# A mixture-of-experts kernel beside a spectral filter: the data's low part last in each product, and three low parts a unit formed by VectorE instead of GpSimd

## The chip, the cores and the metric

The kernel runs on one core of a Trainium2 chip. The metric is the time on the device in microseconds (us), the median of several runs. Five engines have queues of their own and run side by side: TensorE (PE; its weight loads are listed as PEld), VectorE (DVE), ScalarE (ACT), GpSimd (POOL) and SyncE (SP, which here issues transfers). An engine works through its queue in order.

## The reference

The input x has 2048 tokens of 512 numbers. The result is x + A(layernorm(x)) + B(layernorm(x)). A is a filter in the frequency domain, B a mixture of 8 experts in which each token uses all 8 (K = 8), weighted by its gates:

```python
def A(x, w_r, w_i):
    X = fft.rfft2(x) * (w_r + 1j * w_i)
    return fft.irfft2(X, s=(S, D))

def B(xt, wg, w1, w2):               # xt (2048, 512), w1 (8, 512, 1792), w2 (8, 1792, 512)
    gates = softmax(xt @ wg)         # top 8 of 8, normalised again
    h = gelu(einsum("nd,edf->nef", xt, w1))
    y = einsum("nef,efd->ned", h, w2)
    return einsum("ne,ned->nd", gates, y)
```

All arrays are fp32.

## The kernel before

**Exactness.** TensorE multiplies fp32r numbers, which carry fewer bits than fp32. Each operand is therefore split into a high part, rounded to fp32r, and a low part, the rest: ScalarE casts the high part, then VectorE or GpSimd subtracts it from the source (`high` and `low`, L983 and L988, for data; `split`, L682, for weights). A product of two operands takes three passes: low weights by high data, high by low, high by high. The tuple `PASSES` (L44) holds the order (1, 0), (0, 1), (0, 0), where 1 is the low part, the weights' index comes first and the data's second. `PASSES1` (L45) is (0, 0), (1, 0), (0, 1).

**Prologue.** The hidden dimension of each expert is cut into 7 chunks of 256, 56 chunks in all. The first two go through a plain scheme in the first 120 us (`mm1`, L708, with `PASSES1`, and `mm2`, L729, with `PASSES`), while the layer norm, the gates and the operands of the rest are prepared.

**Units.** The other 54 chunks are taken two at a time (27 pairs, index c), and the tokens in two halves (index i): 54 units, numbered u, in a loop (L1302). "Even" and "odd" units are those with i = 0 and i = 1. Each unit does both layers for its pair by Strassen's scheme in Winograd's form: 7 block products a layer instead of 8, with sums of blocks as operands. A block product (`product`, L946) is 256 x 256 weights by 256 x 512 data: for each of two column halves m, three passes by two k, so 12 matmuls of 512 columns. Each column half has a PSUM bank of its own. Three pairs of banks, A, B and C, take the results. Some products start afresh, others add to what is in the bank, and must wait until the result before has been read.

`layer1` (L992) is a generator for the first layer of a unit. It also finishes the unit before: it forms the weighted hidden blocks and their sums, and their high and low parts (tile hs, four buffers), that the second layer of that unit needs. `layer2` (L1134) does the seven products of the second layer, of the unit before, in the order b22, T3, b11, b21, T1, T4, T2, each followed by an addition of the result into acc on VectorE (`into`). T3 adds to b22's bank pair C, b21 to b11's bank pair B, and T4 to T1's bank pair C, each behind that addition. Hidden blocks and their sums lie in five buffers of the tile c (`tmp`, L975): o11, o21, o22 and o12 are those of the unit before, h11, s, h22 and h12 those of this one.

**Order.** A unit is seven steps n, each with one product of layer 1 (first `next(one)`), one of layer 2 (`next(second)`), and the small work between. Every instruction on TensorE, VectorE, ScalarE and GpSimd is pinned to the order in which it is written (`pin`). `weights(n)` puts the preparation of the next weights there: ScalarE casts them (tiles ua, us of layer 1, va, vs of layer 2), GpSimd forms their low parts and the sums of blocks (tiles s and raw), each a two-input instruction of 512 columns. The filter A is cut into small chunks that are put in between by `slot_pe` and `slot_dve`: matmuls into psf and VectorE work on the tiles Y, A, B, C, D of line 438 (names that PSUM's banks share by chance).

The data of layer 1 come from device memory (`xin`, tile xr), high and low parts together.

Before the change, in a unit: VectorE forms the low parts of T3 (step 0), T4 and T2 (step 2) and of b22 (step 6). GpSimd forms those of T1 (step 0), b21 (step 1) and b11 (step 3), by `low(..., True)`.

Of the kernel before, what the change touches and what calls it, by code (L numbers as in the profile page):

```python
# [19 lines left out]
P = 128  # L20
# [99 lines left out]
def body(ctx: ExitStack, tc: tile.TileContext, io):  # L120
    plain_order, strict, pinned = False, False, {}

    def pin(ins):
        if strict:
            engine = ins.ins.engine
            last = pinned.get(engine)
            if last is ins.ins:
                return ins
            if last is not None:
                tc.add_manual_dep(  # L130
                    ins.ins, last.name,
                    mybir.DependencyInfo(mybir.DependencyClass.NoSync, mybir.DependencyReason.DATA), reason="layout",
                )
            pinned[engine] = ins.ins
        return ins
# [593 lines left out]
    def mm2(q, t, w2, h):  # L729

        e = ORDER[2 * q] // NC
        for j in range(TB // P):
            js = slice(j * P, (j + 1) * P)
            p2 = ps2.tile([P, D], F32, name="p2")
            n = 0
            for f in range(2 * NFT):
                for hw, hh in PASSES:
                    nc.tensor.matmul(p2, h[f][:, hh, js], w2[f][:, hw], start=(n == 0), stop=(n == 6 * NFT - 1))
                    n += 1
            b = t * 4 + j  # L740
            early()
            nc.vector.scalar_tensor_tensor(
                acc[:, b, :], p2, cw[:, b, e : e + 1], acc[:, b, :], op0=ALU.mult, op1=ALU.add
            )
            tick()
# [199 lines left out]

    def product(pt, w, x, start):  # L946

        for m in range(2):
            n = 0
            for hw, hx in PASSES:  # L950
                for k in range(2):
                    pin(nc.tensor.matmul(
                        pt[:, m, :], w[:, hw, k, m * P : (m + 1) * P], x[:, hx, k, :], start=(start and n == 0), stop=(n == 5),
                        skip_group_check=not start,
                    ))
                    n += 1

    def bank(name):
        return pq.tile([P, 2, TB], F32, name=name)
# [21 lines left out]
    def less(dst, a, b):  # L981
        pin(nc.vector.tensor_sub(dst, a, b))
# [5 lines left out]
    def low(hs, n, src, pool=False):  # L988
        op = (nc.gpsimd if pool else nc.vector).tensor_tensor(hs[n][:, 1], src, r32(hs[n][:, 0]), op=ALU.subtract)
        return pin(op).ins  # L990

    def layer1(c, i, w, hs, old):  # L992

        last = (c, i) == (N2 - 1, 1)
        first = c == 0 and i == 0
        e = [ORDER[N1 + 2 * c + j] // NC for j in range(2)]
        cb = {}
        oh, o11, o21, o22, o12, oweigh = tuple(old) or (None,) * 6

        def weigh(dst, src, fh, nh):  # L1000
            g = cb[e[fh]][:, nh : nh + 1, :].to_broadcast([P, 2, TB])
            pin(nc.vector.tensor_mul(dst, src, g))

        if (c, i) in fetched:
            cb[e[0]] = fetched.pop((c, i))
        else:
            cb[e[0]] = gate(e[0], i)
        X = bank("C" if (c, i) == (0, 1) else "B")
        x = xin("b11", i)
        product(X, w["a11"], x, True)  # L1010
        Z = bank("A")
        copy_of(Z, X)
        if first:
            B = bank("C")
            product(B, w["s3"], xin("T3", i), True)
        yield
        if (c, i) == (0, 1):
            high(oh, "T3", o12)
        if old:
            low(oh, "T3", o12)  # L1020
        yield
        if old:
            oweigh()
            less(o22, o22, o11)
            high(oh, "T1", o11)
            low(oh, "T1", o11, True)
        yield

        if first:
            product(Z, w["s2"], xin("T2", i), False)  # L1030
            s = copy_of(tmp(), Z)
        product(X, w["a12"], xin("b21", i), False)
        gelu(X)
        yield
        if old:
            high(oh, "b21", o21)
            low(oh, "b21", o21, True)
        h11 = tmp()
        if first:
            plus(s, B, s)  # L1040
        weigh(h11, X, 0, 0)
        yield
        if old:
            less(o12, o22, o21)
        yield

        if not first:
            product(Z, w["s2"], xin("T2", i), False)
            s = copy_of(tmp(), Z)
        if e[1] not in cb:  # L1050
            cb[e[1]] = gate(e[1], i)
        yield
        if old:
            high(oh, "T4", o12)
        yield
        if old:
            low(oh, "T4", o12)
            high(oh, "T2", o22)
            low(oh, "T2", o22)
        yield  # L1060

        product(Z, w["s1"], xin("T1", i), False)
        h22 = copy_of(tmp(), Z)
        if first:
            Y = bank("B")
            product(Y, w["a22"], xin("T4", i), True)
            plus(h22, B, h22)
            gelu(h22)
            plus(s, Y, s)
            high(hs, "b11", h11)  # L1070
        yield
        if first:
            weigh(h22, h22, 1, 1)
            low(hs, "b11", h11, True)
            high(hs, "b22", h22)
        yield
        if not first:
            high(hs, "b11", h11)
            low(hs, "b11", h11, True)
        yield  # L1080

        product(Z, w["s4"], xin("b22", i), False)
        if first:
            with tc.issue_after(last_x[0]):
                fetched[0, 1] = gate(e[0], 1)
        gelu(Z)
        if first:
            low(hs, "b22", h22)
        yield
        h12 = tmp()  # L1090
        weigh(h12, Z, 0, 1)
        yield
        if last:
            high(hs, "b12", h12)
            low(hs, "b12", h12, True)
        else:
            less(h11, h12, h11)
        yield

        if not first:  # L1100
            B = bank("B")
            product(B, w["s3"], xin("T3", i), True)
            plus(h22, B, h22)
            gelu(h22)
        yield
        if not first:
            weigh(h22, h22, 1, 1)
        yield
        if not first:
            high(hs, "b22", h22)  # L1110
        yield

        if not first:
            product(B, w["a22"], xin("T4", i), False)
            plus(s, B, s)
        gelu(s)
        yield
        if not last:
            less(h12, h22, h12)
        if not first:  # L1120
            low(hs, "b22", h22)
        yield
        if last:
            weigh(s, s, 1, 0)
            high(hs, "b21", s)
            low(hs, "b21", s)
        elif not first:
            high(hs, "T3", h12)
        if first:
            last_pool[0] = nc.gpsimd.tensor_copy(mark[:, :1], h12[:, 0, :1]).ins  # L1130
        old[:] = hs, h11, s, h22, h12, lambda: weigh(s, s, 1, 0)
        yield
# [169 lines left out]
    for u in range(2 * N2):  # L1302
# [45 lines left out]
        for n in range(7):  # L1348
            next(one)
            if u and not end and (n == 2 or n == 0 and u > 1 or n == 5 and chunks and (chunks[0][0] or chunks[0][2] < 1.35)):  # L1350
                if slot_pe() and n == 5:
                    slot_dve()
            if n == 4 and u % 2 == 0 and 0 < u and not end and chunks and not chunks[0][0] and chunks[0][2] < 1.35:
                slot_pe()
            if i:
                weights(n)
            if u == 1 and n == 0:
                next(second)
            next(one)
            if n not in (2, 3):  # L1360
                slot_dve()
            if u != 1 or n:
                next(second, None)
            if u and n == 3 and not end:
                slot_pe()
            if n in (2, 3):
                slot_dve()
            next(one)
            if not i:
                weights(n)  # L1370
            if end:
                if n == 0:
                    finals(1)
                if n == 2:
                    split(both[0][:, :, :, FC:], raw2.rearrange("p (k f) -> p k f", k=2), nc.gpsimd)
                if 3 <= n < 6:
                    name = ("a11", "a12", "a22")[n - 3]
                    dh, fh = (int(digit) - 1 for digit in name[1:])
                    pin(nc.scalar.copy(both[fh][:, :, :, dh * FC : (dh + 1) * FC], r32(w2q[name])))
                for b in ((), (), (12, 13), (14, 15), (4, 5), (6,), (7,))[n]:  # L1380
                    rs[b] = rows_of(b, 1)
# [54 lines left out]
```

## Time and profile before

| | before |
|---|---|
| median of 3 runs | 2309.81 us (2309.43 to 2309.86) |
| profiled execution, time | 2307.58 us |
| its span on the core | 2305.8 us |
| granted TensorE clock | 1.00 |
| PE busy | 2291.2 us, 10478 matmuls |
| DVE busy | 1870.1 us, 1753 instructions |
| ACT busy | 1121.5 us |
| POOL busy | 1410.0 us, 790 instructions |
| low parts hs on GpSimd | 161, mean 2.659 us |
| low parts hs on VectorE | 214, mean 1.515 us |

In a row of the timeline stand the start (us from the span's start), the length in us, the engine, the line, the operation, the tiles (written <- read), shapes, and how many instructions the row merges. In square brackets stands how long the engine was idle before, and what ended that. In a list of waits stand the total, the number and the longest. In a row by stretches stand the stretch, its length, and the busy time and number of instructions of PE, PEld, DVE, ACT and POOL, then the clock, the share of the DMA engines' time and GB/s. An engine counts as busy from an instruction's start to its end. Matmuls overlap (one lasts 0.39 us, the next starts after 0.23 us), so a short stop of TensorE is only partly idle time there. Nearly all instructions carry line 105, that of the wrapper that records them, and are told apart by their tiles.

### The profile page before, as it was taken

What the parts mean: (1) busy time and instruction counts of PE and PEld (TensorE: products, weight loads), DVE (VectorE), ACT (ScalarE), POOL (GpSimd) and SP (SyncE); (2) the same over time, 40 slices, a digit from 0 to 9 for tenths busy, and PEclk for the clock granted to TensorE, in tenths of its full rate; (3) what the DMA queues carried; (4) which work ended last, traced back from release to release, by engine and by line L of the source; (5) the groups of instructions that cost most, each with busy time, mean ns of one, the idle gap of its engine ahead of it and who ended that gap; (6) DMA issues with size and microseconds to landing.
All of it is one profiled execution on the core that took longest, in us unless ns stands there. A gap on an engine that the chain in (4) does not pass through costs nothing.

```text
span 2305.8 us, 27834 instructions
## 1 busy us (share of the span) xinstructions
PE 2291.2 (99%) x10478; PEld 1892.7 (82%) x10478; DVE 1870.1 (81%) x1753; ACT 1121.5 (49%) x1559; POOL 1410.0 (61%) x790
## 2 busy tenths in 40 slices
PE   9999999999999999999999999999999999999999
PEld 7778888888888888888888888888888888888887
DVE  8766778798889988877777777898889888876776
ACT  6546554444444445444444554454444445444442
POOL 3355566667566766755555556676667666745563
PEclk9999999999999999999999999999999999999999
DMA  7896876676677667688877776767676666688773
GB/s 251 306 360 241 292 254 246 231 257 232 246 267 261 236 249 262 235 293 295 283 273 244 257 248 232 257 212 249 224 260 223 237 228 240 248 309 282 280 275 133
DMA packets 123717, 588.57 MB, mean 255 GB/s; under 512 B 13600, under 2 KB 16288, under 8 KB 66880
## 3 DMA queue, kind: packets, MB, share of 16 engines
q1 hardware_dynamic: 122784, 574.06, 69.9%
q10 hardware_dynamic: 800, 12.74, 1.4%
q8 instruction: 83, 1.36, 0.2%
q14 instruction: 50, 0.41, 0.1%
HBM read 550.96 MB, written 48.37 MB: 260 GB/s over the span
## 4 chain that ended last, share of the span: by engine, by line
PE 87%; DVE 10%; issue 1%; POOL 1%; ACT 1%; DMA 1%; ACTq 0%; DVEq 0%; POOLq 0%
PE B L105 34%; PE C L105 23%; PE A L105 23%; PE psf L438 4%; DVE c L105 4%; PE p L105 2%; DVE Y L438 2%; DVE acc L105 2%; DVE hs L105 2%; PE psf L105 1%; DVE B L438 1%; DVE xr L105 1%; DMA xs_T<-Y 0%; POOL us L105 0%; POOL raw L105 0%
## 5 line engine op out<-in xcount | busy, mean ns | idle before, releaser
L105 POOL TENSOR_TENSOR hs<-c,hs 128x1024 fp32r<-128x1024 f32 x161 | 428.1, 2659 | 346.3 <-ACT hs L105 339.3
L105 ACT CAST hs<-c 128x1024 fp32r<-128x1024 f32 x375 | 394.0, 1052 | 147.6 <-DVE c L105 73.2
L105 PE MATMUL A<-xr,us 128*128 128x512 f32 x1920 | 463.3, 390 | 0.0
L105 PE MATMUL C<-hs,vs 128*128 128x512 f32 x1884 | 457.7, 391 | 2.9 <-DVE hs L105 2.8
L105 PE MATMUL B<-xr,ua 128*128 128x512 f32 x1884 | 455.3, 391 | 0.5 <-POOL us L105 0.5
L105 PEld LDWEIGHTS A<-xr,us 128*128 128x128 f32 x1920 | 359.8, 188 | 74.6
L105 PEld LDWEIGHTS C<-hs,vs 128*128 128x128 f32 x1884 | 351.9, 188 | 80.3 <-ACT vs L105 6.0
L105 PEld LDWEIGHTS B<-xr,ua 128*128 128x128 f32 x1884 | 353.5, 188 | 76.6 <-DVE c L105 1.9
L105 DVE TENSOR_TENSOR hs<-c,hs 128x1024 fp32r<-128x1024 f32 x214 | 320.6, 1515 | 6.2 <-ACT hs L105 6.1
L105 DVE TENSOR_TENSOR c<-c 128x1024 f32<-128x1024 f32 x212 | 319.8, 1508 | 0.1
L105 DVE TENSOR_TENSOR acc<-C,acc 128x1024 f32<-128x1024 f32 x207 | 252.1, 1218 | 70.1 <-PE C L105 69.9
L105 PE MATMUL B<-hs,va 128*128 128x512 f32 x1248 | 301.5, 390 | 0.0
L105 PEld LDWEIGHTS B<-hs,va 128*128 128x128 f32 x1248 | 233.5, 188 | 48.5 <-DVE c L105 0.2
L105 DVE TENSOR_TENSOR acc<-B,acc 128x1024 f32<-128x1024 f32 x103 | 125.9, 1223 | 164.2 <-PE B L105 163.7
L105 ACT ACTIVATE c<-c 128x1024 f32<-128x1024 f32 x108 | 114.7, 1062 | 256.4 <-DVE c L105 256.1
L105 ACT COPY c<-A 128x1024 f32<-128x1024 f32 x108 | 109.7, 1016 | 234.1 <-PE A L105 201.2
L105 DVE TENSOR_TENSOR c<-c,cwb 128x1024 f32<-128x1024 f32 x108 | 182.3, 1688 | 37.5 <-ACT c L105 37.5
L105 POOL TENSOR_TENSOR ua<-raw,ua 128x512 fp32r<-128x512 f32 x81 | 132.5, 1636 | 130.1 <-ACT ua L105 130.1
L105 POOL TENSOR_TENSOR va<-raw,va 128x512 fp32r<-128x512 f32 x81 | 142.9, 1764 | 86.7 <-ACT va L105 86.7
L105 PE MATMUL C<-hs,va 128*128 128x512 f32 x660 | 162.1, 394 | 2.4 <-DVE acc L105 2.0
L105 PE MATMUL A<-hs,vs 128*128 128x512 f32 x636 | 153.4, 390 | 0.0
L105 PE MATMUL B<-xr,us 128*128 128x512 f32 x636 | 153.2, 390 | 0.0
(188 smaller groups left out, 2964.9 us busy)
## 6 DMA issues: line engine op xcount, KB each, us to landing
xr<-xs_T SPq DMA_DIRECT2D x212, 1024.0 KB, 6.4
xr<-xs_b SPq DMA_DIRECT2D x161, 1024.0 KB, 5.8
cwb<-cwd SPq DMA_DIRECT2D x124, 256.0 KB, 6.0
raw<-in_wa SPq DMA_DIRECT2D x27, 1024.0 KB, 4.9
raw<-in_wb SPq DMA_DIRECT2D x27, 1024.0 KB, 4.8
xs_T<-Y SPq DMA_DIRECT2D x8, 1024.0 KB, 6.2
us<-xfd SPq DMA_DIRECT2D x32, 256.0 KB, 3.2
D<-mbd SPq DMA_DIRECT2D x32, 256.0 KB, 5.3
```

The source lines that it names most:

```text
L105: return lambda *args, **kw: self.order(made(*args, **kw))
L438: return pin(fn(*args, **kw))
```

## The change

- `product` no longer takes all passes of one column half before the other. It takes the passes (0, 0) and (1, 0), both with the data's high part, over both column halves (8 matmuls), and then the pass (0, 1), with the data's low part, over both (4 matmuls). The number of matmuls stays.
- `mm2` takes the passes in the order of `PASSES1`, which also has the data's low part last.
- The low parts of T1, b21 and b11 are formed on VectorE. That of T1 moves from step 0 to the end of step 1, behind less(o12). That of b21 moves from step 1 to step 2, where `layer1` has one more `yield` and the loop one more `next(one)`: it stands behind the addition of the product b11 and ahead of the filter's chunk and of the low parts of T4 and T2. That of b11 keeps its place in step 3. In the first unit (b11) and the last (b12) GpSimd keeps one low part each.

```diff
             for f in range(2 * NFT):
-                for hw, hh in PASSES:
+                for hw, hh in PASSES1:
                     nc.tensor.matmul(p2, h[f][:, hh, js], w2[f][:, hw], start=(n == 0), stop=(n == 6 * NFT - 1))
...
     def product(pt, w, x, start):
 
-        for m in range(2):
-            n = 0
-            for hw, hx in PASSES:
-                for k in range(2):
-                    pin(nc.tensor.matmul(
-                        pt[:, m, :], w[:, hw, k, m * P : (m + 1) * P], x[:, hx, k, :], start=(start and n == 0), stop=(n == 5),
-                        skip_group_check=not start,
-                    ))
-                    n += 1
+        for passes in (((0, 0), (1, 0)), ((0, 1),)):
+            for m in range(2):
+                for hw, hx in passes:
+                    for k in range(2):
+                        pin(nc.tensor.matmul(
+                            pt[:, m, :], w[:, hw, k, m * P : (m + 1) * P], x[:, hx, k, :],
+                            start=start and hw == hx == k == 0, stop=hx == k == 1, skip_group_check=not start,
+                        ))
...
             high(oh, "T1", o11)
-            low(oh, "T1", o11, True)
         yield
...
             high(oh, "b21", o21)
-            low(oh, "b21", o21, True)
         h11 = tmp()
...
             less(o12, o22, o21)
+            low(oh, "T1", o11)
         yield
...
             high(oh, "T4", o12)
+        yield
+        if old:
+            low(oh, "b21", o21)
         yield
         if old:
             low(oh, "T4", o12)
...
             high(hs, "b11", h11)
-            low(hs, "b11", h11, True)
+            low(hs, "b11", h11)
         yield
...
             if u and n == 3 and not end:
                 slot_pe()
+            if n == 2:
+                next(one)
             if n in (2, 3):
                 slot_dve()
             next(one)
```

## The prediction

> **What bounds the kernel now.** First the page's table of engines.
>
> ```profile
> PE 2291.2 (99%) x10478; PEld 1892.7 (82%) x10478; DVE 1870.1 (81%) x1753; ACT 1121.5 (49%) x1559; POOL 1410.0 (61%) x790
> ```
>
> TensorE is busy 99% of the span and no matmul is added or removed, so the change can win only what TensorE still waits, and lose by making it wait more. So the second view is the list of what TensorE waited for.
>
> ```profile
> PE C L105 <- DVE hs L105: 2.8, 8, 0.4
> PE C L105 <- DVE acc L105: 2.0, 4, 0.6
> ...
> PE B L105 <- DVE hs L105: 0.5, 1, 0.5
> PE B L105 <- POOL us L105: 0.5, 1, 0.5
> ```
>
> Two waits recur: for a low part (hs) that VectorE forms, and for a read of bank C (acc) by VectorE. The same list for weight loads counts the places where the second is at its limit:
>
> ```profile
> PEld C L105 <- DVE acc L105: 8.2, 18, 1.0
> ```
>
> Both waits name VectorE, which is idle 19% of the span. So the third view is the timeline, where the waits lie. The low part first: the layer 2 product with b22 starts, stops after two matmuls and goes on when the low part is there.
>
> ```profile
> 1827.55 2.89 PE L105 MATMUL B<-xr,ua 128*128 128x512 f32 x12
> 1830.28 0.62 PE L105 MATMUL C<-hs,vs 128*128 128x512 f32 x2
> 1831.26 0.93 PE L105 MATMUL C<-hs,vs 128*128 128x512 f32 x3 [0.36 <-DVE hs L105]
> ```
> ```profile
> 1828.80 2.31 DVE L105 TENSOR_TENSOR hs<-c,hs 128x1024 fp32r<-128x1024 f32 x1
> ```
>
> A product takes 2.73 us (1827.55 to 1830.28), so a matmul follows the last after 0.23. The third was due at 1830.28 + 0.46 = 1830.74 and began at 1831.26: 0.52 lost. The low part took 2.31 where it can take 1.21, as these rows show (least, median, greatest):
>
> ```profile
> L105 DVE TENSOR_TENSOR hs<-c,hs x214: 1207/1217/2327, 139.7 to 2280.0; 128x1024 fp32r<-128x1024 f32 x107
> L105 POOL TENSOR_TENSOR hs<-c,hs x161: 2389/2407/3427, 137.8 to 2265.3; 128x1024 fp32r<-128x1024 f32 x161
> ```
> ```profile
> L105 DVE TENSOR_TENSOR c<-A,cwb x54: 1208/1224/1228, 141.9 to 2262.5; 128x1024 f32<-128x1024 f32 x54
> ```
>
> A VectorE instruction with one input in PSUM (c<-A,cwb) is always 1.21 to 1.23. One with both inputs in SBUF can be held by 1.1, about one GpSimd instruction of 512 columns (1.3). The next rows show both engines in an even unit, behind its third layer 2 product, where VectorE has no idle time:
>
> ```profile
> 1805.70:1818.00 12.30, 12.30 (x55) 10.16 (x55) 12.29 (x9) 5.17 (x6) 7.57 (x4) 1.00 0.62 224
> ```
> ```profile
> 1801.39 1.66 DVE L105 TENSOR_TENSOR c<-c 128x1024 f32<-128x1024 f32 x1
> 1805.71 1.23 DVE L105 TENSOR_TENSOR acc<-B,acc 128x1024 f32<-128x1024 f32 x1 [2.66 <-PE B L105]
> 1806.85 1.22 DVE L438 TENSOR_TENSOR Y<-Y 128x1024 f32<-128x1024 f32 x1
> 1807.98 3.46 DVE L105 TENSOR_TENSOR hs<-c,hs 128x1024 fp32r<-128x1024 f32 x2
> 1811.37 1.21 DVE L105 TENSOR_TENSOR acc<-B,acc 128x1024 f32<-128x1024 f32 x1
> 1812.50 3.27 DVE L438 TENSOR_TENSOR B<-Y 128x1024 f32<-128x1024 f32 x1
> 1815.70 1.21 DVE L105 TENSOR_TENSOR c<-A,cwb 128x1024 f32<-128x1024 f32 x1
> 1816.83 1.21 DVE L438 TENSOR_TENSOR Y<-Y 128x1024 f32<-128x1024 f32 x1
> 1817.96 1.21 DVE L105 TENSOR_TENSOR acc<-C,acc 128x1024 f32<-128x1024 f32 x1
> ```
> ```profile
> 1807.36 1.87 POOL L105 TENSOR_TENSOR va<-raw,va 128x512 fp32r<-128x512 f32 x1 [1.77 <-ACT va L105]
> 1812.30 2.40 POOL L105 TENSOR_TENSOR hs<-c,hs 128x1024 fp32r<-128x1024 f32 x1 [3.07 <-ACT hs L105]
> 1814.65 2.28 POOL L105 TENSOR_TENSOR va<-raw,va 128x512 fp32r<-128x512 f32 x1
> 1816.90 2.30 POOL L105 TENSOR_TENSOR raw<-raw 128x512 f32<-128x512 f32 x1
> ```
> ```profile
> 1816.43 2.89 PE L105 MATMUL B<-xr,us 128*128 128x512 f32 x12
> 1819.23 3.02 PE L105 MATMUL C<-hs,va 128*128 128x512 f32 x12
> ```
>
> The two engines take turns. B<-Y waits until the low part of b11 (1812.30, GpSimd) is done at 1814.70 and takes 3.27, 2.06 over its 1.21; GpSimd's va then waits for B<-Y, so it takes 2.28. A GpSimd instruction of 512 columns costs VectorE up to 1.3, one of 1024 up to 2.2, and nothing beside a PSUM instruction. The acc read of bank C ends at 1819.17 and the T4 product, which adds into that bank, starts at 1819.23, 0.07 after it was due (1816.43 + 2.73 = 1819.16). VectorE is here just in time.
>
> **The change part by part.**
>
> Order of the passes (L946). The low part is needed at matmul 9, not 3: six matmuls, 1.37 us, later. All eight waits of the first row are shorter than that and go, if VectorE comes no more than 0.8 later there. Each costs 0.52 and some 0.1 until the pace is back: 8 x 0.62 = 5.0 us. Bounds: 2.8 (the row) and 5.3 (each as long as the longest, 0.4 idle, with 0.16 that the row leaves out under the matmuls' ends and the 0.1). In the first units one wait for hs (0.5) goes and one for us, needed two matmuls later, nearly so: 1.0 us. In mm2 (L729) the low part is needed one matmul, 0.23, later; four tiles bound it at 0.9, I take 0.4. A product switches its bank three times instead of once. For what that costs a row with no switch at all stands below (rivals); I take nothing.
>
> GpSimd's three low parts a unit go: 161 x 2.41 = 388 us of its time at least, all but the few of the first and last unit. Its other work keeps its order and moves forward only where it stood behind them, since the casts on ScalarE release most of it.
>
> VectorE gets them: three a unit, each 1.13 in a row of instructions (1806.85 to 1807.98). What this does to TensorE is decided in the stretch above, walked again with the new order and these durations:
> ```profile
> 1803.02 1.02 ACT L105 COPY c<-A 128x1024 f32<-128x1024 f32 x1 [3.54 <-PE A L105]
> ...
> 1812.12 0.62 ACT L105 CAST va<-raw 128x512 fp32r<-128x512 f32 x1
> ```
> - 1805.71 acc<-B, as before, to 1806.85. Then the low part of b21 (new), to 1807.98. GpSimd's va, ready at 1807.36, takes its turn, to 1809.28.
> - Y<-Y to 1810.41, the low parts of T4 and T2 to 1812.67. Before they ended at 1811.37, since va fell on them once as well. So acc<-B is 1.30 later and ends at 1813.80.
> - The second va, released by the cast at 1812.74, no longer stands behind a GpSimd low part: it runs to 1814.04. B<-Y runs from there to 1815.17 instead of 1815.70. GpSimd's raw<-raw takes its turn, to 1816.47.
> - The low part of b11 (new) to 1817.60, c<-A,cwb to 1818.73. GpSimd's vs, whose cast (0.62 again) ends at 1817.1, runs from 1817.60 to 1818.90 and holds Y<-Y, which ends at 1820.03.
> - acc<-C starts at 1820.03 instead of 1817.96. T4 starts 2.07 later: **2.1 us lost in this unit**.
>
> The sum says the same: two low parts add 2.26, the GpSimd low part that went gave 2.06 back, and GpSimd's other instructions, now earlier, fall on VectorE's SBUF instructions and take 1.9 again. Not every unit is so full. Where the filter's step is light, VectorE has idle time in that stretch:
>
> ```profile
> 459.77 1.23 DVE L105 TENSOR_TENSOR c<-A,cwb 128x1024 f32<-128x1024 f32 x1 [2.54 <-ACT A L105]
> ```
>
> There the low part of b11 costs nothing. I take the 18 places of the weight loads' row as those at the limit, and between 2.1 and 0.2 (if GpSimd's turns all fall beside PSUM instructions: 2.26 less 2.06) 1.5 each, nearer to the walked one: 18 x 1.5 = 27 us. Bounds: 18 x 0.2 = 4 us; 18 x 2.1 = 38, with up to 0.5 more at the next product of each, whose bank B is read behind the same queue, 47. Below nothing: these waits gone too, which is 4 us (2.0 us idle by the row, and as much again hidden under the matmuls' ends).
>
> The low part of T1 comes later than on GpSimd, behind less(o12) instead of before it. It keeps a c buffer of five, which ScalarE's copy of bank A takes next. In the walked unit less(o12) started at 1801.39; undisturbed it ends its turn at 1802.52, T1 at 1803.7, the copy (1.02) at 1804.7. The product that adds to bank A starts at about 1805.5, when acc<-B becomes due. 0.8 is spare: nothing, at most one turn of GpSimd late (0.5) in half of the units.
>
> Sum: -5.0 - 1.0 - 0.4 + 27 = +20.6 on the profiled execution's 2307.6 gives 2328. The median of the runs is 2.2 above that execution: **2330 us**.
>
> **The rivals.** Faster: the queue gets shorter, not longer. A low part costs 1.2 on VectorE instead of 2.4 on GpSimd, VectorE loses fewer turns, and the late places stay as late as now. By the walk it holds if GpSimd's turns fall beside PSUM instructions in most of the 18 units; the price is then -6.4 + 4 at the worst, and -6.4 - 4 at the best: 2299 to 2307, or 2303. For it: the 2.06 that one GpSimd low part cost. Against it: VectorE 12.29 of 12.30 busy with 2.26 more to do. The Trainium skill (GPSIMD Engine Reference, 4.1 Engine selection) sides with it: elementwise work belongs on VectorE, about twice as fast for two inputs. The rows agree on the factor (2407 to 1217 ns), but the rule looks at an instruction, not at the queue it joins.
>
> No change: the growth is some 0.3 a place, 18 x 0.3 = 5, which cancels the 6.4: about 2309.
>
> Slower by another place: the copy of bank A waits for T1's low part. Where one turn of GpSimd falls before it, the product is 0.5 late; in 27 units 13 us, without growth at T4 2317.
>
> Bank switches: one row shows a product without any.
>
> ```profile
> 93.41 2.73 PE p L105 x12
> ```
>
> It takes 2.73 like those with one, so a switch costs under 0.01; 750 products with two more bound it at 7 us. The Trainium skill (TensorE: Matmul & The Clock Gate, A second HAM failure mode: psum-queue depth-cycling) reports kernels whose cycling through banks made TensorE pause and its clock fall. Here the clock is 1.00 in the window above with a switch in each product; I give it 0.02.
>
> **How the numbers follow.** Slower at T4 0.60, by T1 or the banks 0.07, no change 0.13, faster 0.20. About 0.2%, 4.6 us, is what a measurement can tell from no change. The range runs from the faster rival's 2303 to the upper bound: -5 + 47 gives 2352. Within the likeliest case alone it is 2315 to 2352. Faster 0.20, same 0.13, slower 0.67.
>
> **What would show it.** Right: no stop behind the second matmul of C<-hs,vs; VectorE's busy time up, by at most 161 x 1.14 = 184 us, since turns lost to GpSimd's low parts come back; GpSimd's down by about 400; waits of PE C for DVE acc of 1 to 2 us in even units of the stages in which the filter runs on VectorE alone, as the filter's own instructions show by stage (TensorE's first):
>
> ```profile
> 200.00:360.00 160.00, 23.32 (x174) 22.96 (x174) 21.24 (x42) 24.10 (x72) 1.00 0.72 252
> 360.00:1000.00 640.00, 0.00 (x0) 0.00 (x0) 99.75 (x100) 8.81 (x38) 1.00 0.70 251
> ...
> 1400.00:2020.00 620.00, 0.00 (x0) 0.00 (x0) 102.65 (x91) 8.88 (x37) 1.00 0.68 239
> ```
>  Wrong: those waits stay at 0.1, or VectorE's idle time before acc<-B is still there and T4 starts on time.

## The result: slower by 1.1%, at the place that was named

| | before | after |
|---|---|---|
| median of the runs beside each other | 2309.84 us (2309.43 to 2311.79) | 2334.82 us (2332.88 to 2337.94) |
| profiled execution, time and span | 2307.58, 2305.8 us | 2332.88, 2331.1 us |

The ratio is 1.0106, with a 95% interval of 1.0094 to 1.0118. The forecast was 2330 us. The table of engines of the kernel after:

```profile
PE 2294.3 (98%) x10478; PEld 1897.2 (81%) x10478; DVE 1983.3 (85%) x1912; ACT 1118.6 (48%) x1559; POOL 1027.5 (44%) x631
```

VectorE has 159 instructions more and 113.2 us more busy time; GpSimd 382.5 us less. The waits of TensorE, and the one of the weight loads that grew:

```profile
PE C L105 <- DVE acc L105: 26.6, 14, 3.1
PE B L105 <- DVE c L105: 1.5, 2, 1.1
...
PE A L105 <- ACT c L105: 1.2, 4, 0.4
```
```profile
PEld C L105 <- DVE acc L105: 32.9, 15, 3.5
```

The waits for low parts (hs) are gone, and the wait for the read of bank C went from 2.0 to 26.6 us. To see all stops, also those hidden under the matmuls' ends, take from the trace each matmul's start less the start of the one before less 0.2275 us, the usual distance. The sums of what is above 0.02 us, between 198 and 2262 us, in us, by the matmul that came late:

| stop ahead of | before | after |
|---|---|---|
| T4's first matmul (C<-hs,va) | 3.6 (13 places) | 29.0 (15) |
| b22's third and fourth (C<-hs,vs) | 5.5 (9) | 0 |
| a product of layer 1 into B (B<-xr,ua, first) | 0 | 2.4 (6) |
| a product of layer 1 into A (A<-xr,us, first) | 0 | 1.8 (4) |
| all, with the rest | 11.8 | 39.6 |

The difference of 27.8 here and the 2.8 us that are won ahead of 198 us make 25.0, against 25.3 between the spans; from 2262 us to the end the two kernels take the same time.

Now the stretch that the prediction walked, in the kernel after (the same even unit, 22.94 us later):

```profile
1828.65 1.23 DVE L105 TENSOR_TENSOR acc<-B,acc 128x1024 f32<-128x1024 f32 x1 [1.79 <-PE B L105]
1829.79 1.22 DVE L105 TENSOR_TENSOR hs<-c,hs 128x1024 fp32r<-128x1024 f32 x1
1830.92 2.33 DVE L438 TENSOR_TENSOR Y<-Y 128x1024 f32<-128x1024 f32 x1
1833.17 2.35 DVE L105 TENSOR_TENSOR hs<-c,hs 128x1024 fp32r<-128x1024 f32 x2
1835.44 1.21 DVE L105 TENSOR_TENSOR acc<-B,acc 128x1024 f32<-128x1024 f32 x1
1836.57 1.56 DVE L438 TENSOR_TENSOR B<-Y 128x1024 f32<-128x1024 f32 x1
1838.06 2.31 DVE L105 TENSOR_TENSOR hs<-c,hs 128x1024 fp32r<-128x1024 f32 x1
...
1842.56 1.21 DVE L105 TENSOR_TENSOR acc<-C,acc 128x1024 f32<-128x1024 f32 x1
```
```profile
1830.48 1.69 POOL L105 TENSOR_TENSOR va<-raw,va 128x512 fp32r<-128x512 f32 x1 [6.99 <-ACT va L105]
1835.76 1.30 POOL L105 TENSOR_TENSOR va<-raw,va 128x512 fp32r<-128x512 f32 x1 [3.59 <-ACT va L105]
1837.02 2.27 POOL L105 TENSOR_TENSOR raw<-raw 128x512 f32<-128x512 f32 x1
```
```profile
1839.37 2.88 PE L105 MATMUL B<-xr,us 128*128 128x512 f32 x12
1843.83 3.02 PE L105 MATMUL C<-hs,va 128*128 128x512 f32 x12 [1.58 <-DVE acc L105]
```

From acc<-B to acc<-C it is 13.91 us (1828.65 to 1842.56); before it was 12.25, the walk said 14.32. Two more low parts stand in the queue, and Y<-Y (held by the first va, 1.12), B<-Y (by the second, 0.35) and b11's low part (by raw<-raw, 1.10) still lose 2.6 to GpSimd's turns. The walk had these three, at 1.30, 0.24 and 1.30, and a fourth of 0.17. T4 is due 2.73 after 1839.37, at 1842.10, and starts 1.73 late. Of the 15 late places 11 lie in even units (0.7 to 2.4 us, 20.1 in sum), three in odd units (2.8, 3.3 and 2.8 us), and one is 0.1.

Behind some of the long waits TensorE's granted clock fell. Stretches with the clock, and T4's product behind three of the waits:

```profile
816.00:828.00 12.00, 8.88 (x28) 6.77 (x27) 10.38 (x9) 3.13 (x4) 4.26 (x3) 0.72 0.27 95
1764.00:1768.00 4.00, 4.00 (x12) 3.15 (x13) 2.88 (x3) 1.06 (x1) 0.00 (x0) 0.62 0.72 289
```
```profile
820.60 5.49 PE L105 MATMUL C<-hs,va 128*128 128x512 f32 x12 [3.12 <-DVE acc L105]
1684.90 3.02 PE L105 MATMUL C<-hs,va 128*128 128x512 f32 x12 [2.25 <-DVE acc L105]
1763.88 4.61 PE L105 MATMUL C<-hs,va 128*128 128x512 f32 x12 [2.25 <-DVE acc L105]
```

The second is what the product takes behind a wait at full clock; the others take 2.5 and 1.6 more: some 4 us of the 25.

### The profile page after: what moved, and what is told of

Its sections match the earlier page's. It is cut to its first block, busy times and chain, and to the rows that moved or that the text cites. A ratio compares the mean times of both kernels' runs of the same rounds, so it can differ in the third digit from the quotient of the medians.

```text
span 2331.1 us, 27690 instructions
## 1 busy us (share of the span) xinstructions
PE 2294.3 (98%) x10478; PEld 1897.2 (81%) x10478; DVE 1983.3 (85%) x1912; ACT 1118.6 (48%) x1559; POOL 1027.5 (44%) x631
## 4 chain that ended last, share of the span: by engine, by line
PE 84%; DVE 11%; issue 2%; DMA 1%; ACT 1%; POOL 1%; ACTq 0%; POOLq 0%; DVEq 0%
PE B L105 33%; PE C L105 23%; PE A L105 21%; DVE hs L105 4%; PE psf L438 4%; PE p L105 3%; DVE Y L438 2%; DVE c L105 2%; DVE acc L105 2%; PE psf L105 1%; DMA us<-xfd 1%; DVE B L438 1%; DMA raw<-in_wa 0%; DVE A L438 0%; ACT c L105 0%
## 5 line engine op out<-in xcount | busy, mean ns | idle before, releaser
L105 DVE TENSOR_TENSOR hs<-c,hs 128x1024 fp32r<-128x1024 f32 x373 | 530.2, 1432 | 17.3 <-ACT hs L105 17.1
L105 DVE TENSOR_TENSOR c<-c 128x1024 f32<-128x1024 f32 x212 | 307.8, 1452 | 0.1
L105 POOL TENSOR_TENSOR ua<-raw,ua 128x512 fp32r<-128x512 f32 x81 | 117.4, 1450 | 369.2 <-ACT ua L105 355.3
L105 PE MATMUL C<-hs,va 128*128 128x512 f32 x660 | 166.0, 401 | 26.6 <-DVE acc L105 26.6
L105 PEld LDWEIGHTS C<-hs,va 128*128 128x128 f32 x660 | 124.0, 192 | 58.7 <-DVE acc L105 32.9
L105 DVE TENSOR_TENSOR c<-c,cwb 128x1024 f32<-128x1024 f32 x108 | 136.5, 1264 | 37.6 <-ACT c L105 37.6
```

The costliest lines, as they stand in the source:

```text
L105: return lambda *args, **kw: self.order(made(*args, **kw))
```

## The experiments

Two theories of the loss. By the turns: VectorE has room for three more low parts a unit, and what decides is which GpSimd instruction then falls on which VectorE instruction ahead of a read that TensorE waits for. By the load: VectorE's queue is simply too long, and each low part taken off it shortens the waits.

**The order alone.** The kernel before, with the diff's `product` and `mm2`:

```diff
-for m in range(2):
-    for hw, hx in PASSES:
...
+for passes in (((0, 0), (1, 0)), ((0, 1),)):
+    for m in range(2):
+        for hw, hx in passes:
```

> The kernel before with the new order of passes alone (product and mm2); all low parts stay where they were. Queue theory (the loss comes from the low parts of b21 and b11 standing in VectorE's full stretch ahead of the addition that the T4 product waits for): the waits behind the second matmul of C<-hs,vs go, 5.0 us, and 1.4 in the first 200 us; the waits of T4 stay near the 5 us of before. 2309.8 - 6.4 = 2303. Order rival (more bank switches or a later low part cost TensorE time by themselves): 2310 or more, up to the 2335 of the changed kernel.

2308.14 us, ratio 0.9993 (0.9984 to 1.0002), where 2303 was expected: a miss. The stops at b22 went (5.5 us to none), but 3.1 and 1.0 us now stand before the first and second matmul of the product a12, in nine odd units, and three products a11 lose 0.9 more than before. The waits, and a place where an even unit ends and an odd one begins:

```profile
PE C L105 <- DVE acc L105: 2.0, 4, 0.6
PE B L105 <- ACT A L105: 1.7, 8, 0.2
```
```profile
1827.98 2.31 DVE L105 TENSOR_TENSOR hs<-c,hs 128x1024 fp32r<-128x1024 f32 x1
1830.22 1.21 DVE L105 TENSOR_TENSOR acc<-A,acc 128x1024 f32<-128x1024 f32 x1
1831.52 1.00 ACT L105 COPY A<-B 128x1024 f32<-128x1024 f32 x1 [1.80 <-DVE acc L105]
1832.57 3.03 PE L105 MATMUL B<-xr,ua 128*128 128x512 f32 x12 [0.22 <-ACT A L105]
```

A chain: b22's low part is held by GpSimd, so VectorE reads bank A late, so ScalarE's copy from B to A is late, and TensorE may not yet add into B. Before, the same copy was as late, but TensorE had been stopped at b22 already:

```profile
1832.34 1.00 ACT L105 COPY A<-B 128x1024 f32<-128x1024 f32 x1 [1.80 <-DVE acc L105]
...
1833.63 0.62 PE L105 MATMUL B<-xr,ua 128*128 128x512 f32 x2
```

The copy ended at 1833.34, 0.29 before that product started. In the first of the two traces the product starts 0.05 behind the copy's end, so 0.24 was to spare. At b22 TensorE had lost 0.62 (3.35 from 1830.28 to 1833.63, instead of 2.73). Without these 0.62 a12 has to be 0.38 late, and it is: due 2.73 behind b22's start at 1829.46, it starts at 1832.57 instead of 1832.19. (The row's 0.22 is idle time; the rest lies under the end of the matmul before.)

**The low parts alone.** The kernel after, with the old `product` and `mm2`: the same lines the other way round.

> The changed kernel with the old order of passes in product and mm2; the three low parts stay on VectorE. Queue theory: the waits of PE C for acc stay at about 27 us, and the waits for low parts behind the second matmul come back where VectorE is late there: 2334.8 plus 0 to 6, so 2335 to 2341. Order rival: without the new order the time goes back to about 2310.

2335.16 us, ratio 1.0109 (1.0095 to 1.0123), as with both. The order takes nothing off the loss. Of the stops at b22, 5.5 us before, one of 0.6 is left here without the new order: in the changed kernel they go by the moved low parts already.

**One low part back on GpSimd, each in turn.** The kernel after, with one of these:

```diff
 high(hs, "b11", h11)
-low(hs, "b11", h11)
+low(hs, "b11", h11, True)                  # b11 back
...
 high(oh, "b21", o21)
+low(oh, "b21", o21, True)                  # b21 back; the one in step 2 goes
...
 high(oh, "T1", o11)
+low(oh, "T1", o11, True)                   # T1 back; the one in step 1 goes
```

> The changed kernel with one low part, that of b11 (step 3), back on GpSimd. Queue theory with turns: in the walked unit VectorE does 1.13 less but loses a turn of 2.06 on the filter's instruction again; b11's low part then also keeps GpSimd's other instructions back, so that they fall beside PSUM instructions as before. The addition comes about 0 to 0.3 later than in the kernel before instead of 2.1: the waits of T4 fall from 29 us to about 6, 2334.8 - 23 = 2312, less 2 to 4 that a clock drop behind long waits costs: 2308 to 2312. Load rival (each of the two low parts in the stretch counts alike, by its 1.13 on VectorE): half of the loss comes back, about 2322.

> The changed kernel with b21's low part back on GpSimd in step 1; those of T1 and b11 stay on VectorE where the change put them. Queue theory: b11's low part alone in the stretch. By the walk the addition that T4 waits for comes 0.75 later than before the change, where both make it 2.1 later: T4's waits 12 to 16 us, 2315 to 2321. If the stretch has no other time to spare, b21 alone (2320.8 with b11 back on GpSimd) and b11 alone cost alike, and their costs of 13 and about 10 add up to the changed kernel's 25. Turn rival (GpSimd's turns alone make the loss, the work on VectorE is free): near 2309.

> The changed kernel with T1's low part back on GpSimd in step 0; b21's and b11's stay on VectorE. Queue theory: T1's low part stands in time that VectorE has to spare; the waits of T4 stay at about 29 us, and only the waits of the product that adds to bank A for ScalarE's copy (1.8 + 0.4 us in the changed kernel) can go: 2331 to 2335. Load rival (each low part counts alike): a third of the loss comes back, 2326 or less.

b11 back: 2320.8 us, ratio 1.0048 (1.0035 to 1.0060), the rival's number. b21 back: 2318.68, ratio 1.0036 (1.0022 to 1.0050), the number met, but with waits at another place (below). T1 back: 2322.81, ratio 1.0053 (1.0039 to 1.0067), the number of the load, where the turns were thought to leave 2331 to 2335. One at a time they give back 14, 16 and 12 us, 42 of a loss of 25: they don't add up.

T1 was the surprise. The even units' waits at T4 stayed (1.7 and 2.4), but the odd units' three, 8.8 us, were gone. The odd unit of the longest wait, first in the kernel after, then with T1 back on GpSimd:

```profile
800.86 1.21 DVE L105 TENSOR_TENSOR hs<-c,hs 128x1024 fp32r<-128x1024 f32 x1
802.19 1.02 ACT L105 COPY c<-A 128x1024 f32<-128x1024 f32 x1 [4.01 <-DVE hs L105]
803.80 1.30 POOL L105 TENSOR_TENSOR ua<-raw,ua 128x512 fp32r<-128x512 f32 x1 [3.94 <-ACT ua L105]
803.88 1.23 DVE L105 TENSOR_TENSOR acc<-B,acc 128x1024 f32<-128x1024 f32 x1 [1.80 <-PE B L105]
805.06 2.32 POOL L105 TENSOR_TENSOR s<-s,raw 128x512 f32<-128x512 f32 x1
806.15 2.32 DVE L438 TENSOR_TENSOR Y<-Y 128x1024 f32<-128x1024 f32 x1
808.39 4.53 DVE L105 TENSOR_TENSOR hs<-c,hs 128x1024 fp32r<-128x1024 f32 x2
819.33 1.21 DVE L105 TENSOR_TENSOR acc<-C,acc 128x1024 f32<-128x1024 f32 x1
```
```profile
800.80 1.02 ACT L105 COPY c<-A 128x1024 f32<-128x1024 f32 x1 [3.02 <-PE A L105]
802.41 1.30 POOL L105 TENSOR_TENSOR ua<-raw,ua 128x512 fp32r<-128x512 f32 x1 [2.67 <-ACT ua L105]
803.49 1.23 DVE L105 TENSOR_TENSOR acc<-B,acc 128x1024 f32<-128x1024 f32 x1 [2.67 <-PE B L105]
803.67 1.31 POOL L105 TENSOR_TENSOR s<-s,raw 128x512 f32<-128x512 f32 x1
805.98 1.21 DVE L438 TENSOR_TENSOR Y<-Y 128x1024 f32<-128x1024 f32 x1
807.12 3.45 DVE L105 TENSOR_TENSOR hs<-c,hs 128x1024 fp32r<-128x1024 f32 x2
815.02 1.21 DVE L105 TENSOR_TENSOR acc<-C,acc 128x1024 f32<-128x1024 f32 x1
```

With T1's low part on VectorE the copy c<-A waits for it (in the second kernel for TensorE alone). ScalarE's casts stand behind the copy, GpSimd's ua and s behind the casts: s starts 1.18 behind acc<-B instead of 0.18. There it misses its cover under that PSUM instruction: it waits for b21's low part, takes 2.32 instead of 1.31, and Y<-Y waits for it. The turns after it shift likewise, and acc<-C comes 15.45 behind acc<-B instead of 11.53. TensorE loses 3.3 by a copy that was itself in time.

**T1's low part alone on VectorE.** The kernel after, with b21's and b11's back on GpSimd.

> The kernel after with the low parts of b21 and b11 back on GpSimd, in the steps where they were before; only T1's is on VectorE, at the end of step 1. Theory: T1's low part shares that place with GpSimd's low part of b21, is held by it, and ScalarE's copy of bank A waits for it in odd units, as in the run with b21 alone moved back (17 places of 0.5 to 0.6 us): 2314 to 2318, with waits of PE A for ACT c of 6 to 9 us and no waits at T4. Rival: the copy was late there only because VectorE's queue was full through b11's low part as well; then 2307 to 2310.

2319.1 us, ratio 1.0039 (1.0026 to 1.0051); the waits here and, second, with b21 alone back:

```profile
PE A L105 <- ACT c L105: 7.9, 17, 0.5
```
```profile
PE A L105 <- ACT c L105: 7.8, 17, 0.5
```

Now the copy itself is late, in 17 odd units, as the prediction's rival at this place had it: GpSimd's low part of b21 holds that of T1 (3.42 us instead of 1.21, at 1695.49 us). One low part on VectorE, the least that any of these kernels adds to it, costs 9 us; by the load it should have cost least.

**Most of GpSimd's turns taken away.** The kernel after, but GpSimd writes zeros as the weights' low parts, so the results lack these parts. Its sums s and raw stay.

```diff
-split(to[n], src.rearrange("p (k f) -> p k f", k=2), nc.gpsimd)
+main_act[0] = pin(nc.scalar.copy(to[n][:, 0], src.rearrange("p (k f) -> p k f", k=2))).ins
+pin(nc.gpsimd.memset(r32(to[n][:, 1]), 0.0))
```

> The changed kernel, in which GpSimd fills the low parts of the weights ua, us, va and vs with zeros instead of subtracting (so the results lack the weights' low parts); its sums s and raw stay. GpSimd's share of the loss: seven of eleven two-input instructions a unit no longer read SBUF and take no turn from VectorE. Queue theory with turns: VectorE has 2.3 more to do in the stretch but loses one turn (raw) instead of three: T4's waits fall from 29 to below 8 us, 2300 to 2314. If VectorE's own work makes the loss and the turns are only shifted about: 2325 or more.

2299.98 us, ratio 0.9955 (0.9941 to 0.9968). The table of engines, and one place in its timeline:

```profile
PE 2286.4 (99%) x10478; PEld 1895.1 (82%) x10478; DVE 1868.8 (81%) x1912; ACT 1117.6 (49%) x1559; POOL 556.7 (24%) x631
```
```profile
1810.19 0.99 POOL L105 MEMSET vs<- 128x512 f32 x2 [1.44 <-PE C L105]
1810.90 1.21 DVE L438 TENSOR_TENSOR Y<-Y 128x1024 f32<-128x1024 f32 x1
```

VectorE does the same 1912 instructions in 114.5 us less. So its three more low parts a unit fit; what doesn't fit is that work and GpSimd's turns together. A GpSimd instruction that only writes holds nothing: Y<-Y begins during the second MEMSET and takes its 1.21. In the whole trace 122 VectorE instructions of 1024 columns with both inputs in SBUF overlap with MEMSETs alone, and none takes more than 1.23. (The MEMSETs are also shorter, 0.53 against 1.30, so GpSimd's other work moves as well.) The Trainium skill (SBUF — State Buffer, SBUF: two separate sides) states just this: a VectorE instruction with two SBUF inputs shares a lock with a GpSimd instruction that reads SBUF, and whoever is second waits for the whole of the other. These rows agree.

**Other places for the low parts.** The kernel after, with b21's behind T1's at the end of step 1 and b11's in step 4:

```diff
 low(oh, "T1", o11)
+low(oh, "b21", o21)                        # the one in step 2 goes
...
-low(hs, "b11", h11)
...
+if not first:
+    low(hs, "b11", h11)
 if last:
     high(hs, "b12", h12)
```

> The changed kernel with two low parts moved on VectorE: that of b21 to the end of step 1, right behind T1's, into the 1.8 to 2.7 us in which VectorE waits for the product b11; that of b11 to step 4, behind the addition of the product T1 and ahead of less(h11). Nothing is added to the stretch, and GpSimd's low part of b11 (2.06 in the walked unit) is gone from it. Queue theory: the waits of T4 fall to nearly none, those for low parts stay away: between 2296 and 2304, better than both kernels. Load rival (VectorE has too much work in a unit, wherever it stands): the waits only move, to the products b21, a22 or b22, and the time stays above 2320.

2327.97 us, ratio 1.0077 (1.0064 to 1.0090): a miss. The waits at T4 were gone, and another had come:

```profile
PE B L105 <- DVE c L105: 23.1, 26, 1.7
```

The queue was as long behind T4 as it had been ahead of it, and the next read, of the bank that the product a22 adds to (plus(h22, B)), was late. Then the same with b11's on GpSimd in step 3:

```diff
 high(hs, "b11", h11)
+low(hs, "b11", h11, True)
...
-if not first:
-    low(hs, "b11", h11)
```

> The changed kernel with b21's low part on VectorE at the end of step 1 (behind T1's) and b11's low part on GpSimd in step 3, as before the change. The run with both moved on VectorE showed that b11's low part in step 4 only shifts the wait from the T4 product to the product a22, behind plus(h22): the full stretch reaches from step 2 to step 6 of even units. Queue theory: only step 1 has time to spare, and here nothing stands in the stretch that did not stand there before the change: waits as in the run with the order alone, about 12 us, so 2303 to 2309. Load rival (VectorE's work in a unit counts, wherever it stands: two of the three low parts stay on it): about two thirds of the loss, 2325.

2307.74 us, ratio 0.9991 (0.9982 to 1.0000), as expected: two of three low parts can move and cost nothing, where T1's alone cost 9 us. In an odd unit those two follow each other without a turn of GpSimd's:

```profile
1843.34 2.35 DVE L105 TENSOR_TENSOR hs<-c,hs 128x1024 fp32r<-128x1024 f32 x2
```

**Towards a version that beats both.** In the kernel just told, and in the one with the order alone, VectorE reads bank A before it forms b22's low part:

```diff
 if not last:
     less(h12, h22, h12)
+yield
 if not first:
     low(hs, "b22", h22)
-yield
```

> The kernel with the low parts of T1 and b21 at the end of step 1 on VectorE and that of b11 on GpSimd (2307.7), and in addition the low part of b22 is moved behind the addition of the product T2, so that VectorE reads bank A first. Theory: TensorE's short stops at the product a12 (B<-xr,ua, 0.37 and 0.11 at 9 to 11 places) come from ScalarE's copy into bank A, which waits for that read, which is late behind b22's low part. With the read first they go, and the low part still comes before matmul 9 of b22's product: 4 to 5 us less, 2303 to 2304. Rival: the low part of b22 then comes late for matmul 9, and the stop is only moved, as it was when the passes alone were reordered: 2307 to 2309.

> The kernel before with the new order of the passes (2308.1), and in addition the low part of b22 behind the addition of the product T2. Theory, as in the run beside it: the stops at the product a12 (4.1 + 1.5 us in all) go, 2303 to 2304. Rival: the stop moves to matmul 9 of b22's product or to another product, 2307 to 2309.

2314.55 us, ratio 1.0016 (1.0008 to 1.0025), and 2335.79, ratio 1.0111 (1.0095 to 1.0126): both missed. The stops at a12 went in both, but in the first T1's low part came late for the copy of bank A: 10.0 us of stops at 16 products, in even units (not in odd ones, as the expectation below for the last run has it). In the second one an odd unit shows:

```profile
1855.68 3.12 POOL L105 TENSOR_TENSOR hs<-c,hs 128x1024 fp32r<-128x1024 f32 x1 [0.21 <-ACT hs L105]
1856.47 3.41 DVE L438 TENSOR_TENSOR Y<-Y 128x1024 f32<-128x1024 f32 x1
1859.80 1.21 DVE L105 TENSOR_TENSOR acc<-C,acc 128x1024 f32<-128x1024 f32 x1
```

GpSimd's low part of T1 now falls on Y<-Y, which takes 2.2 longer (with the order alone it starts beside the read of bank C, behind Y<-Y), and that read makes T3's product late: 26.8 us in 16 places. Nothing had been added to VectorE's work, and one swap costs as much as the whole change. That is the case that the load can't explain. Last, the first of the two with T1's low part one instruction earlier:

```diff
-less(o12, o22, o21)
 low(oh, "T1", o11)
+less(o12, o22, o21)
 low(oh, "b21", o21)
```

> The kernel with T1's and b21's low parts at the end of step 1 on VectorE, b11's on GpSimd and b22's behind the addition of T2 (2314.6), and in addition T1's low part ahead of less(o12) instead of behind it. Theory: what is left there of new stops is ScalarE's copy of bank A, which waits for T1's low part in odd units (A<-xr,us, 8.4 and 1.9 us of stops in 16 and 17 places); one VectorE instruction earlier, 1.13 us, is more than the longest of these stops (0.9), so they go: 2303 to 2306, under the kernel before (2310.5 on that chip). Rival: some GpSimd instruction falls on VectorE in the new order and the stop shows up at the next product whose bank is read from the same queue, 2310 to 2316.

**2304.12 us, ratio 0.9978 (0.9969 to 0.9987)**: faster than both kernels. Its waits:

```profile
PE B L105 <- DVE c L105: 2.0, 2, 1.7
PE C L105 <- DVE acc L105: 2.0, 4, 0.6
```

The stops between 198 and 2262 us sum to 8.3 (before: 11.8), with none that recurs at a12 or at the copy of bank A. GpSimd still forms the low part of b11 here; no run shows an order in which VectorE forms all three, GpSimd does all its other work and the kernel is not slower.

## Why the prediction was right, and where its terms were not

- **T4, +27 for 18 places of 1.5.** The place was right, and in the even units the mechanism too, but there the term was too large: 20.2 - 3.6 = 16.6 us, 11 places at 1.8 on average. That the whole is 29.0 - 3.6 = 25.4, near the 27, is luck: 8.8 us lie in three odd units, 2.9 each, which were not forecast and came by T1.
- **The walked unit, 2.07.** Measured 1.66 (13.91 less 12.25). The walk's turns of the first va on Y<-Y, the second va on B<-Y and raw<-raw on b11's low part fell just there, 0.3 shorter in sum; the last, vs on the second Y<-Y for 0.17, did not fall. Here the mechanism was predicted turn by turn.
- **Order, -5.0 and -1.4.** The step that failed is "all eight waits go: 8 x 0.62". They went (5.5), but behind them the copy A<-B had only 0.24 to spare, and 4.1 came back at a12 and 0.9 at a11. Alone the order gave 0.07%, with an interval that includes no change at all; the first 198 us gave 0.9 of the 1.4 that was forecast there. Inside the change it gave nothing that can be told: without it all but 0.6 of the stops at b22 go as well, and the medians are 2334.82 with it and 2335.16 without (in the profiled executions the first 198 us gave 2.8 with it and 0.2 without). The prediction did not ask what was late next for this stop, and the row of the copy stood in its own trace.
- **T1's low part, nothing, or 13 by the rival.** Worth 12 us in the change. Both looked at the copy of bank A and whether it was in time. It was, nearly (1.8 us at A<-xr,us); the cost went through the casts behind it on ScalarE to GpSimd's turns. The rival's way was the one with b21's low part on GpSimd (7.9 and 7.8 us above).
- **Bank switches, nothing.** The order alone, with all of them, lost nothing: held. The bound of 7 us was too low by its own row: two more switches in 750 products, at less than 0.01 each, make up to 15.
- **The likeliest case, 2315 to 2352.** The lower end doesn't follow from the terms: with 4 us at T4 and the gains of 6.4 it is 2307.
- **VectorE's busy time up by at most 184, GpSimd's down by about 400.** 113.2 and 382.5: held.
- **The clock.** Some 4 us came from a clock drop that no step had. It is most of the 4.7 by which the profiled execution grew more (25.3) than the sum of the terms (20.6).
- **The faster rival** (2299 to 2307 if GpSimd's turns fall beside PSUM instructions) was not the case of this change, but its condition was the right one: with most of the turns away it was 2300. The rule of the Trainium skill beside it (GPSIMD Engine Reference, 4.1 Engine selection: elementwise work belongs on VectorE) is borne out here per instruction (1217 against 2407 ns) and not by the change.

## What to carry to other kernels

Where two engines take turns, a queue's length is not the sum of its instructions: walk it with the other engine's instructions at their own release times, and again when anything upstream of those releases moves, a copy on ScalarE included. Ask of every stop that goes what was second latest at the next product; its spare time bounds the gain. Three moved low parts cost 25 us in one order; two of them were free, or part of a small gain, in others. Single moves don't add up, so try the places and not only the engine.

## What was not expected of the hardware

TensorE's clock fell to about half (granted 0.50 from 820 to 826 us and from 1765 to 1768.4; a matmul every 0.43 us instead of 0.23) behind waits of 3.12 and 2.25 us, for 8 to 12 matmuls, and not behind others of the same length: the products at 1684.90 and 1763.88 above both stand behind 2.25, and only the second is slow. The Trainium skill (TensorE: Matmul & The Clock Gate, Part 1) tells of windows of some 3.4 us that run freely, and of a clock that is halved behind an idle one. That equal waits act differently agrees with windows that run freely; that 2.25 us of idleness could be enough is less than such a window. Even 2.01 us were enough in the kernel with the order and b22's low part behind the read: there T3's product takes 4.49 to 4.60 us instead of 3.04 behind 2.01 us of idleness in four places (799, 956, 1466 and 1861 us), and 3.04 behind 2.02 in a fifth (405 us). No run here settles where the limit lies.
